# Weight blocks taken in pairs, and one home for both mixed inputs, in an attention and channel-mix kernel

## The chip, the cores and the metric

The kernel runs on one core of a Trainium2 chip. The metric is the device time in microseconds of one execution. The engines are TensorE (PE; its weight loads are PEld), VectorE (DVE), ScalarE (ACT), GpSimd (POOL) and SyncE (SP), which here issues nearly all DMAs from one queue, in order.

## The reference

Two stages. The first is attention for 4 batches, 8 heads, 768 rows and head dimension 64. The scores have a distance bias per head; a row sees the first 8 columns and the 96 columns up to itself. The second stage takes the 512 attention outputs of a row as x:

```
xk = mu_k * x + (1 - mu_k) * x_prev        # x_prev: the row before
xr = mu_r * x + (1 - mu_r) * x_prev
k  = max(xk @ w_k, 0)                      # w_k 512 x 1024
v  = (k * k) @ w_v                         # w_v 1024 x 512
r  = 1 / (1 + exp(-(xr @ w_r)))            # w_r 512 x 512
out = r * v
```

The weights arrive as 64-bit floating point and everything else as 32-bit.

## The kernel before

The 3072 rows are 24 tiles of 128. Each step takes one tile: scores, a maximum and an exponential per head, a sum and its reciprocal (L363, L364 on VectorE), normalisation on GpSimd (L367), a transpose (on TensorE, L404, for the first nine tiles; by VectorE and DMA after that), and the product with v (L425). A step has four slots; the program counts them as `4 * step + hp`. The second stage takes chunks of two tiles, 12 in all. A chunk is a generator with 40 pieces, and each slot asks for five of them, so TensorE alternates between attention and the chunk of some tiles before (the first chunk begins late in step 3). When the last attention step is done, the remaining pieces run back to back.

**The weights.** They are 20 blocks of 128 rows and 512 columns in the order w_k (8), w_r (4), w_v (8). A block goes through three steps.

- `weight_load` (L149): a DMA of the 64-bit words, 512 KB, into a home. The home is a buffer that has another use later: xk_hi, xr_hi, xk_lo, xr_lo (the mixed x), kk_hi and kk_lo (the squared k, two blocks in each), and the three t4k buffers. A home that is taken a second time must have been read out first.
- `weight_begin` (L168): the conversion to 32-bit words. One multiplication, on ScalarE for even blocks (L177) and on GpSimd for odd ones (L175), and then three integer operations on VectorE (L178, L179, L180), the last of which reads the home for the last time.
- `weight_split` (L182): a rounded high part by ScalarE or GpSimd (L187) and the low part by a subtraction on VectorE (L189 before the first output product exists, L192 behind it). The low part takes a buffer of the pool `wl`; the word's buffer comes free with that.

The first chunk multiplies plain 32-bit words (L495 for kp, L474 for z, L527 for the v products, `vps`). All later chunks use high and low parts, three matmuls for each product (L465 to L467). So the words must be there in time for the first chunk and the splits for the second. `w_due` (L147) lists how many blocks are to be loaded, and how many begun, by the end of each slot; `splits_ok` says how many may be split after each piece of the first chunk's v products.

**The chunk.** `mix` (L436) makes xk and xr for all chunks but the first, each as a high and a low tile; `plain_mix` (L448) makes the first chunk's. The tiles kk and sig of a chunk (L500, L478) share the pool `f2`; sig is what the output DMA (L535) reads. The tile framework gives every buffer of a pool to a new tile when all readers of the old one are done, and it orders the instructions of each engine when the program is built, by its own simulated timeline (L773); it does not reorder at run time. So each engine works through a fixed list.

Of the kernel before, what the change touches and what calls it, by code (L numbers as in the profile page):

```python
# [9 lines left out]
F32 = mybir.dt.float32  # L10
F32R = mybir.dt.float32r
# [23 lines left out]
def tile_biased_attention_channel_mix(ctx: ExitStack, tc: tile.TileContext, qT, kT, v, n_sizes, mu_kr, w_k, w_v, w_r, q_rows, k_rows, v_rows, slopes, out):  # L35
    nc = tc.nc
# [107 lines left out]
    w_steps = [(name, src, k, c) for name, src, kts, n in (("k", w_k, 4, DF), ("r", w_r, 4, DM), ("v", w_v, 8, DM)) for c in range(0, n, 512) for k in range(kts)]  # L144

    w_raw = {}
    w_due = ((2, 3, 4, 5, 6, 6, 7, 7, 8, 8, 9, 9, 10, 11, 12, 13, 14, 16, 18, 20, 20, 20, 20, 20), (0, 1, 2, 3, 4, 4, 5, 5, 6, 6, 7, 7, 8, 8, 9, 10, 11, 12, 14, 16, 18, 20, 20, 20))  # L147

    def weight_load(i):  # L149
        name, src, k, c = w_steps[i]  # L150
        home = w_homes[i]
        if home == "t4k":
            raw = p4k.tile([128, 512, 2], I32, tag="t4k", name=f"w64_{i}")
        elif home[0] == "x":
            raw = f_pool.tile([128, 512, 2], I32, tag=home, name=f"w64_{i}")
        else:
            if home in w_both:
                raw = w_both.pop(home)[:, 1]
            else:
                w_both[home] = f_pool.tile([128, 2, 512, 2], I32, tag=home, name=f"w64_{i}")  # L160
                raw = w_both[home][:, 0]
        nc.sync.dma_start(raw.rearrange("p n w -> p (n w)"), src[k * 128 : (k + 1) * 128, 2 * c : 2 * c + 1024])
        w_raw[i] = raw

    w_both = {}
    w_homes = ["xk_hi", "xr_hi", "xk_lo", "xr_lo", "kk_hi", "kk_hi", "kk_lo", "kk_lo"] + 2 * ["t4k", "t4k", "t4k", "xk_lo", "xr_lo"] + ["kk_lo", "kk_lo"]

    def weight_begin(i):  # L168
        name, src, k, c = w_steps[i]
        raw = w_raw.pop(i)  # L170
        low, top = raw[:, :, 0], raw[:, :, 1]
        word = w_pool.tile([128, 512], I32, tag="wl", name=f"word_{i}")
        w_word[name, k, c] = word.bitcast(F32)
# [6 lines left out]
        vec.scalar_tensor_tensor(word, low, 29, word, op0=ALU.logical_shift_right, op1=ALU.bitwise_or)  # L180

    def weight_split(i):  # L182

        name, src, k, c = w_steps[i]
        word, hi = w_word.pop((name, k, c)), w_hi[name][:, k, c : c + 512]
        lo = w_low[name, k, c] = w_pool.tile([128, 512], F32R, tag="wl", name=f"w{name}_lo_{i}")
        (act.copy if i % 4 < 2 else pool_copy)(hi, word)  # L187
        if not gates:
            vec.tensor_sub(lo, word, hi)  # L189
        else:  # L190
            with tc.issue_after(gates[-1]):
                vec.tensor_sub(lo, word, hi)  # L192
# [240 lines left out]
            act.copy(xt[:, :, 1 + 128 * i : 129 + 128 * i], s["av"].rearrange("p (a q) -> p a q", a=4))  # L433


    def mix(xc, xp, tag, tmp_pool, out_pool):  # L436
        m, m1 = mu[tag]
        tmp = tmp_pool.tile([128, 4, 256], F32, name=f"mix_{tag}", tag="t4k")
        hi = out_pool.tile([128, 4, 256], F32R, name=f"x{tag}_hi", tag=f"x{tag}_hi")
        lo = out_pool.tile([128, 4, 256], F32R, name=f"x{tag}_lo", tag=f"x{tag}_lo")  # L440
        for j in range(4):
            pool.tensor_scalar(tmp[:, j, :], xp[:, j, :], m1[:, j : j + 1], 1.0, op0=ALU.mult, op1=ALU.mult)
            vec.scalar_tensor_tensor(tmp[:, j, :], xc[:, j, :], m[:, j : j + 1], tmp[:, j, :], op0=ALU.mult, op1=ALU.add)
        act.copy(hi, tmp)
        vec.tensor_sub(lo, tmp, hi)
        return hi, lo

    def plain_mix(xc, xp, tag):  # L448

        m, m1 = mu[tag]  # L450
        x = f_pool.tile([128, 4, 256], F32, name=f"x{tag}_0", tag=f"x{tag}_hi")
        for j in range(4):
            act.activation(x[:, j, :], xp[:, j, :], AF.Copy, scale=m1[:, j : j + 1])
            vec.scalar_tensor_tensor(x[:, j, :], xc[:, j, :], m[:, j : j + 1], x[:, j, :], op0=ALU.mult, op1=ALU.add)
        return x

    def channel_mix(xk, xr, out_rows, f_pool, f2_pool, ps_f, first=False, last=False):
        if first:
# [22 lines left out]
        sigs = []  # L481
        for fp in range(4):
            if first:
                weights_go(4 if fp < 2 else 8)
            else:
                splits_go(4 if fp < 2 else 8)
            ps = ps_f.tile([128, 512], F32, name="kp", tag="f")
            for u in range(2):
                f = slice((2 * fp + u) * 128, (2 * fp + u + 1) * 128)
                c = fp // 2 * 512  # L490
                g = slice(f.start - c, f.stop - c)
                o = ps[:, u * 256 : (u + 1) * 256]
# [24 lines left out]
        for i in range(2):  # L517
            c = slice(i * 128, (i + 1) * 128)
            sig = sigs[i][1]
            w = 256 if last and i else 512  # L520
            for o in range(0, 512, w):
                d = slice(o, o + w)
                vp = ps_f.tile([128, 512], F32, name="vps", tag="f")
                for f in range(8):
                    if first:
                        weights_go(13 + f)
                        pe.matmul(vp, kk_all[:, f, c], w_word["v", f, 0], start=f == 0, stop=f == 7)  # L527
                        if i or f > 3:
                            splits_ok[0] = 13 + f if i else 12
                    else:  # L530
                        splits_go(13 + f)
# [81 lines left out]
    def wide():  # L613
        with ExitStack() as g:
# [85 lines left out]
            with tc.For_i(0, B, 1) as b:  # L700
                for c in range(3):
# [7 lines left out]
                    xk = mix(xt[:, :, 1:257], xt[:, :, 0:256], "k", work, work)  # L709
                    xr = mix(xt[:, :, 1:257], xt[:, :, 0:256], "r", work, work)  # L710
# [66 lines left out]
```

## Time and profile before

| | us |
|---|---|
| time, median of 3 runs | 483.69 (482.35 to 485.16) |
| profiled execution | 482.42 |
| its span, first to last instruction | 480.6 |
| TensorE busy in the span | 468.3 |
| VectorE busy | 380.6 |
| ScalarE busy | 283.0 |
| GpSimd busy | 255.5 |

Busy time adds what each engine spends in instructions. Matmuls are pipelined and their ends are modelled, so TensorE's busy time says where it had work rather than how hard it worked. [...] A wait is written as engine, line and tile that waited, an arrow, and what ended the wait.

### The profile page before, as it was taken

How to read it: one execution, taken by the hardware profiler on the slowest of the kernel's cores; microseconds unless marked ns; L12 is line 12 of the kernel's file. 1: busy time of each engine (PE TensorE's matmuls, PEld its weight loads, DVE VectorE, ACT ScalarE, POOL GpSimd, SP SyncE). 2: the span in 40 equal slices, each digit the busy share in tenths (PEclk: the TensorE clock that was granted, in tenths of full speed). 3: DMA queues.
4: the chain of work that ended last, by engine and by line, in shares of the span. 5: the costliest groups of instructions: out<-in, count | busy, mean ns of one | idle time of the engine just before them, and what ended most of it. 6: DMA issues, size and time to landing. Idle time of an engine off the chain costs nothing.

```text
span 480.6 us, 9646 instructions
## 1 busy us (share of the span) xinstructions
PE 468.3 (97%) x3300; PEld 402.7 (84%) x3300; DVE 380.6 (79%) x921; ACT 283.0 (59%) x656; POOL 255.5 (53%) x396
## 2 busy tenths in 40 slices
PE   8979999999999999999999999999999999999996
PEld 6758854788898898898898898898898898898985
DVE  6899999988778968978978968978978968746221
ACT  5996636367669548546738638636748549543220
POOL 7676977537447536737646645737646645303000
PEclk9999999999999999999999999999999999999999
DMA  6999634502422575865775785775775554430001
GB/s 177 309 297 312 234 80 64 144 11 89 110 66 72 155 214 177 225 192 143 192 219 182 230 227 165 219 211 159 195 202 191 172 183 160 160 109 24 22 2 48
DMA packets 42279, 76.20 MB, mean 159 GB/s; under 512 B 5616, under 2 KB 23280, under 8 KB 42224
## 3 DMA queue, kind: packets, MB, share of 16 engines
q1 hardware_dynamic: 42080, 75.52, 53.5%
q8 instruction: 28, 0.46, 0.4%
q14 instruction: 27, 0.22, 0.2%
q10 hardware_dynamic: 144, 0.00, 0.0%
HBM read 54.53 MB, written 20.97 MB: 157 GB/s over the span
## 4 chain that ended last, share of the span: by engine, by line
PE 84%; DVE 8%; POOL 2%; issue 2%; DMA 2%; SPq 0%; ACT 0%; POOLq 0%; DVEq 0%
PE vps L466 9%; PE vps L465 9%; PE vps L467 8%; PE kp L465 8%; PE av L425 8%; PE kp L467 8%; PE kp L466 8%; PE z L465 4%; PE z L466 4%; PE z L467 4%; PE s L327 4%; PE s L328 3%; PE t L404 2%; POOL room L367 2%; PE s L325 2%
## 5 line engine op out<-in xcount | busy, mean ns | idle before, releaser
L367 POOL TENSOR_SCALAR room<-room,r 128x256 f32<-128x256 f32 (+1 forms) x192 | 110.2, 591 | 141.7 <-DVE r L364 72.9
L351 ACT ACTIVATE room<-room,nmax 128x256 f32<-128x256 f32 (+1 forms) x192 | 93.0, 486 | 89.7 <-DVE nmax L350 84.2
L465 PE MATMUL kp<-xk_hi,wk_hi 128*128 128x256 f32 x352 | 99.4, 282 | 0.8 <-DVE kk L506 0.8
L467 PE MATMUL kp<-xk_hi,wk_lo 128*128 128x256 f32 x352 | 98.6, 280 | 0.0
L466 PE MATMUL kp<-xk_lo,wk_hi 128*128 128x256 f32 x352 | 98.2, 279 | 0.0
L350 DVE CUSTOM_DVE_ANT_0 room<-s,pat 128x256 f32<-128x256 f32 (+1 forms) x192 | 68.4, 389 | 3.8 <-PE s L325 2.4
L466 PE MATMUL vps<-wv_lo,kk_hi 128*128 128x512 f32 (+1 forms) x184 | 70.9, 385 | 0.0
L465 PE MATMUL vps<-wv_hi,kk_hi 128*128 128x512 f32 (+1 forms) x184 | 70.8, 385 | 0.0
L467 PE MATMUL vps<-wv_hi,kk_lo 128*128 128x512 f32 (+1 forms) x184 | 70.5, 383 | 0.0
L465 PEld LDWEIGHTS kp<-xk_hi,wk_hi 128*128 128x128 f32 x352 | 66.8, 190 | 1.9 <-DVE kk L506 1.0
L466 PEld LDWEIGHTS kp<-xk_lo,wk_hi 128*128 128x128 f32 x352 | 65.9, 187 | 0.7 <-issue 0.2
L467 PEld LDWEIGHTS kp<-xk_hi,wk_lo 128*128 128x128 f32 x352 | 66.0, 187 | 0.0
L378 DVE STREAM_TRANSPOSE room<-room 128x512 f32<-128x512 f32 x52 | 36.0, 702 | 18.0 <-POOL room L367 18.0
L508 DVE TENSOR_TENSOR kk_lo<-kk,kk_hi 128x512 fp32r<-128x512 f32 x44 | 33.7, 765 | 15.0 <-ACT kk_hi L507 13.5
L507 ACT CAST kk_hi<-kk 128x512 fp32r<-128x512 f32 x44 | 27.1, 617 | 26.7 <-DVE kk L506 26.7
L506 DVE TENSOR_TENSOR kk<-kp,kk 128x512 f32<-128x512 f32 x44 | 30.1, 685 | 14.4 <-ACT kk L502 14.3
L467 PEld LDWEIGHTS vps<-wv_hi,kk_lo 128*128 128x128 f32 x184 | 34.6, 188 | 7.5
L465 PEld LDWEIGHTS vps<-wv_hi,kk_hi 128*128 128x128 f32 x184 | 34.7, 188 | 6.4
L425 PE MATMUL av<-room,va 128*64 128x128 f32 x608 | 39.5, 277 | 0.4 <-ACT room L405 0.4
L466 PEld LDWEIGHTS vps<-wv_lo,kk_hi 128*128 128x128 f32 x184 | 34.5, 188 | 6.1
L425 PEld LDWEIGHTS av<-room,va 128*64 128x64 f32 x608 | 33.9, 136 | 5.7 <-issue 2.9
L327 PE MATMUL s<-kw,qh 128*128 128x256 f32 (+1 forms) x136 | 37.0, 295 | 0.0
(116 smaller groups left out, 1022.3 us busy)
## 6 DMA issues: line engine op xcount, KB each, us to landing
moved<-room SPq DMA_DIRECT2D x26, 512.0 KB, 4.0
room<-moved SPq DMA_DIRECT2D x104, 128.0 KB, 3.0
kraw<-in_kT_dram SPq DMA_DIRECT2D x36, 256.0 KB, 4.0
qraw<-in_qT_dram SPq DMA_DIRECT2D x34, 256.0 KB, 4.0
out_dram<-sig SPq DMA_DIRECT2D x23, 256.0 KB, 3.8
va<-in_v_dram SPq DMA_DIRECT2D x21, 256.0 KB, 3.4
w<-in_w_k_dram SPq DMA_DIRECT2D x8, 512.0 KB, 7.8
w<-in_w_v_dram SPq DMA_DIRECT2D x8, 512.0 KB, 4.3
```

The source lines that it names most:

```text
L327: pe.matmul(o, s["qh"][:, h, :], s["kw"][:, h, c0:256], start=True, stop=False)
L350: vec.tensor_tensor_reduce(out=e[:, :w], in0=o, in1=p[:, h, :], op0=ALU.add, op1=ALU.min, scale=-0.125, scalar=3.0e38, accum_out=s["nmax"] ...
L351: act.activation(e[:, :w], e[:, :w], AF.Exp, bias=s["nmax"][:, h : h + 1], scale=-1.0, accum_out=s["sum"][:, h : h + 1])
L367: pool.tensor_scalar(e[:, :w], e[:, :w], r[:, i : i + 1], 1.0, op0=ALU.mult, op1=ALU.mult)
L378: vec.transpose(dst, src.rearrange("p u (g b j) -> p (u g) b j", b=4, j=32))
L425: pe.matmul(o, vt[:, h * 64 : (h + 1) * 64], g, start=k == 0, stop=k == nb - 1)
L465: pe.matmul(o, sh, mh, start=first, stop=False)
L466: pe.matmul(o, sh, ml, start=False, stop=False)
L467: pe.matmul(o, sl, mh, start=False, stop=last)
L506: vec.tensor_mul(kk, pv, kk)
L507: act.copy(kkh[:, 2 * fp : 2 * fp + 2, :], kk)
L508: vec.tensor_sub(kkl[:, 2 * fp : 2 * fp + 2, :], kk, kkh[:, 2 * fp : 2 * fp + 2, :])
```

## The change

Weights go in ten pairs of blocks. A pair is two neighbouring blocks of rows in the same 512 columns: one DMA of 1 MB, one multiplication and three VectorE operations over 1024 columns, one rounding and one subtraction over 1024 columns. Even pairs take ScalarE for the multiplication and the rounding, odd pairs GpSimd. The pool `wl` has 11 buffers of twice the size, `f2` three instead of four. The mixed x has one tile x_hi of twice the size for the high parts of xk and xr, and one x_lo for the low parts. The pairs' homes are x_hi, x_lo, kk_hi, kk_lo, and then three times x_lo and kk_lo in turn; t4k is no home any more. The lists of due slots and the counts at which the chunks ask for weights are in pairs. The arithmetic is the same.

```diff
-    w_pool = ctx.enter_context(tc.tile_pool(name="wl", bufs=21))
+    w_pool = ctx.enter_context(tc.tile_pool(name="wl", bufs=11))
...
-    f2_pool = fast.enter_context(tc.tile_pool(name="f2", bufs=4))
+    f2_pool = fast.enter_context(tc.tile_pool(name="f2", bufs=3))
...
-    w_steps = [... for c in range(0, n, 512) for k in range(kts)]
+    w_steps = [... for c in range(0, n, 512) for k in range(0, kts, 2)]
...
-    w_due = ((2, 3, 4, 5, 6, 6, 7, 7, 8, 8, 9, 9, 10, 11, 12, 13, 14, 16, 18, 20, 20, 20, 20, 20), (0, 1, 2, 3, 4, 4, 5, 5, 6, 6, 7, 7, 8, 8, 9, 10, 11, 12, 14, 16, 18, 20, 20, 20))
+    w_due = ((1, 2, 2, 3, 3, 3, 3, 4, 4, 4, 5, 5, 5, 6, 6, 7, 8, 9, 10, 10, 10, 10, 10, 10), (0, 1, 1, 2, 2, 2, 2, 3, 3, 3, 4, 4, 4, 5, 5, 6, 7, 8, 9, 10, 10, 10, 10, 10))
+    w_homes = ["x_hi", "x_lo", "kk_hi", "kk_lo"] + 3 * ["x_lo", "kk_lo"]
...
     def weight_load(i):
+        raw = w_raw[i] = f_pool.tile([128, 2, 512, 2], I32, tag=w_homes[i], name=f"w64_{i}")
+        nc.sync.dma_start(raw.rearrange("p k n w -> p k (n w)"), src[k * 128 : (k + 2) * 128, 2 * c : 2 * c + 1024].rearrange("(k p) x -> p k x", k=2))
...
-    w_homes = ["xk_hi", "xr_hi", "xk_lo", "xr_lo", "kk_hi", "kk_hi", "kk_lo", "kk_lo"] + 2 * ["t4k", "t4k", "t4k", "xk_lo", "xr_lo"] + ["kk_lo", "kk_lo"]
...
     def weight_begin(i):
-        word = w_pool.tile([128, 512], I32, tag="wl", name=f"word_{i}")
+        word = w_pool.tile([128, 2, 512], I32, tag="wl", name=f"word_{i}")
...
     def weight_split(i):
-        lo = w_low[name, k, c] = w_pool.tile([128, 512], F32R, tag="wl", name=f"w{name}_lo_{i}")
-        (act.copy if i % 4 < 2 else pool_copy)(hi, word)
+        lo = w_pool.tile([128, 2, 512], F32R, tag="wl", name=f"w{name}_lo_{i}")
+        (act.copy if i % 2 == 0 else pool_copy)(hi, word)
...
-    def mix(xc, xp, tag, tmp_pool, out_pool):
+    def mixes(xc, xp, tmp_pool, out_pool):
+        both = [out_pool.tile([128, 2, 4, 256], F32R, name=f"x_{p}", tag=f"x_{p}") for p in ("hi", "lo")]
+        for i, tag in enumerate("kr"):
...
-    def plain_mix(xc, xp, tag):
+    def plain_mixes(xc, xp):
+        both = f_pool.tile([128, 2, 4, 256], F32, name="x_0", tag="x_hi")
+        for i, tag in enumerate("kr"):
...
-                            splits_ok[0] = 13 + f if i else 12
+                            splits_ok[0] = 6 + (f + 1) // 2 if i else 6
```

## Rows read from the trace of the kernel before

**Rows 1.** Page: engines' busy time, share of the span, instructions.
```profile
PE 468.3 (97%) x3300; PEld 402.7 (84%) x3300; DVE 380.6 (79%) x921; ACT 283.0 (59%) x656; POOL 255.5 (53%) x396
```
**Rows 2.** Windows: us, busy (instructions) of PE, PEld, DVE, ACT, POOL, clock, DMA, GB/s.
```profile
16.00:36.00 20.00, 15.97 (x132) 12.49 (x132) 18.86 (x61) 19.09 (x54) 14.36 (x19) 1.00 1.04 302
36.00:57.00 21.00, 20.98 (x144) 18.26 (x144) 21.00 (x56) 13.77 (x37) 15.42 (x21) 1.00 0.85 277
57.00:75.00 18.00, 18.00 (x94) 9.79 (x93) 17.39 (x28) 9.18 (x16) 14.59 (x16) 1.00 0.54 127
86.00:102.00 16.00, 14.81 (x139) 13.39 (x138) 14.90 (x38) 6.63 (x22) 6.89 (x12) 1.00 0.31 85
...
200.00:250.00 50.00, 50.00 (x386) 45.58 (x385) 41.90 (x99) 28.31 (x72) 27.31 (x41) 1.00 0.70 197
```
**Rows 3.** Waits of PE, whole span: us in total, times, longest.
```profile
PE t L404 <- POOL room L367: 4.0, 5, 1.4
...
PE kp L465 <- DVE kk L506: 0.8, 1, 0.8
...
PE vps L527 <- DVE word L180: 0.5, 1, 0.5
PE av L425 <- ACT room L405: 0.4, 1, 0.4
```
**Rows 4.** Timeline of DVE: start, us, engine, line, operation, tiles, shapes.
```profile
24.55 0.68 DVE L179 SCALAR_TENSOR_TENSOR word<-w,word 128x512 int32<-128x512 int32 x1
25.16 0.16 DVE L363 TENSOR_SCALAR r<-sum 128x4 f32<-128x4 f32 x1
...
43.51 0.66 DVE L180 SCALAR_TENSOR_TENSOR word<-w,word 128x512 int32<-128x512 int32 x1
...
82.21 1.22 DVE L445 TENSOR_TENSOR xk_lo<-mix_k,xk_hi 128x1024 fp32r<-128x1024 f32 x1
83.34 1.22 DVE L445 TENSOR_TENSOR xr_lo<-mix_r,xr_hi 128x1024 fp32r<-128x1024 f32 x1
```
**Rows 5.** Groups: ns min/median/max, then starts; or busy us, mean ns.
```profile
L175 POOL TENSOR_SCALAR word<-w x10: 651/789/1110, 16.8 to 65.7; 128x512 f32<-128x512 f32 x10
L192 DVE TENSOR_TENSOR wv_lo<-word,wv_hi x8: 685/691/822, 93.6 to 99.6; 128x512 fp32r<-128x512 f32 x8
...
L454 DVE SCALAR_TENSOR_TENSOR xk<-x,mus,xk 128x256 f32<-128x256 f32 x4 | 2.7, 702 | 0.0
```
**Rows 6.** SyncE's queue: its waits in all, and the timeline of the loads.
```profile
SPq L162 <- DVE word L180: 9.3, 5, 4.6
...
44.51 12.42 SPq L162 DMA_DIRECT2D w<-in_w_v_dram  x7
```
**Rows 7.** Weight loads from 44 to 58 us, to landing.
```profile
DMA to landing us min/median/max: 3.3/4.1/4.7
```
**Rows 8.** Timeline of POOL.
```profile
48.24 3.48 POOL L367 TENSOR_SCALAR room<-room,r 128x256 f32<-128x256 f32 x4
...
59.01 5.12 POOL L367 TENSOR_SCALAR room<-room,r 128x256 f32<-128x256 f32 x4
```
**Rows 9.** Timeline of PE, first chunk's v products; last column: idle before, releaser.
```profile
73.25 1.98 PE L527 MATMUL vps<-word,kk 128*128 128x512 f32 x4
...
75.89 1.13 PE L527 MATMUL vps<-word,kk 128*128 128x512 f32 x2 [0.55 <-DVE word L180]
```
**Rows 10.** One chunk in the steady part: PE, ACT, SP timelines, and the page's DMA issues.
```profile
223.67 0.40 PE L465 MATMUL z<-wr_hi,xr_hi 128*128 128x512 f32 x1
...
230.35 1.04 ACT L444 CAST xk_hi<-mix_k 128x1024 fp32r<-128x1024 f32 x1
...
241.73 0.43 SPq L535 DMA_DIRECT2D out_dram<-sig  x1
...
249.78 0.59 ACT L502 ACTIVATE kk<-kp 128x512 f32<-128x512 f32 x1
...
out_dram<-sig SPq DMA_DIRECT2D x23, 256.0 KB, 3.8
```

More of the change, by code (lines that the diff above doesn't have):

```diff
@@ L142, in tile_biased_attention_channel_mix @@
     pool.tensor_scalar(mus1, mus, -1.0, 1.0, op0=ALU.mult, op1=ALU.add)
-    w_steps = [(name, src, k, c) for name, src, kts, n in (("k", w_k, 4, DF), ("r", w_r, 4, DM), ("v", w_v, 8, DM)) for c in range(0, n, 512) for k in range(kts)]
+    w_steps = [(name, src, k, c) for name, src, kts, n in (("k", w_k, 4, DF), ("r", w_r, 4, DM), ("v", w_v, 8, DM)) for c in range(0, n, 512) for k in range(0, kts, 2)]
     w_raw = {}
-    w_due = ((2, 3, 4, 5, 6, 6, 7, 7, 8, 8, 9, 9, 10, 11, 12, 13, 14, 16, 18, 20, 20, 20, 20, 20), (0, 1, 2, 3, 4, 4, 5, 5, 6, 6, 7, 7, 8, 8, 9, 10, 11, 12, 14, 16, 18, 20, 20, 20))
+    w_due = ((1, 2, 2, 3, 3, 3, 3, 4, 4, 4, 5, 5, 5, 6, 6, 7, 8, 9, 10, 10, 10, 10, 10, 10), (0, 1, 1, 2, 2, 2, 2, 3, 3, 3, 4, 4, 4, 5, 5, 6, 7, 8, 9, 10, 10, 10, 10, 10))
+    w_homes = ["x_hi", "x_lo", "kk_hi", "kk_lo"] + 3 * ["x_lo", "kk_lo"]
     def weight_load(i):
         name, src, k, c = w_steps[i]
[L151 to L165, printed above, removed]
-    w_homes = ["xk_hi", "xr_hi", "xk_lo", "xr_lo", "kk_hi", "kk_hi", "kk_lo", "kk_lo"] + 2 * ["t4k", "t4k", "t4k", "xk_lo", "xr_lo"] + ["kk_lo", "kk_lo"]
+        raw = w_raw[i] = f_pool.tile([128, 2, 512, 2], I32, tag=w_homes[i], name=f"w64_{i}")
+        nc.sync.dma_start(raw.rearrange("p k n w -> p k (n w)"), src[k * 128 : (k + 2) * 128, 2 * c : 2 * c + 1024].rearrange("(k p) x -> p k x", k=2))
     def weight_begin(i):
@@ L170, in weight_begin @@
         raw = w_raw.pop(i)
-        low, top = raw[:, :, 0], raw[:, :, 1]
-        word = w_pool.tile([128, 512], I32, tag="wl", name=f"word_{i}")
-        w_word[name, k, c] = word.bitcast(F32)
+        low, top = raw[:, :, :, 0], raw[:, :, :, 1]
+        word = w_pool.tile([128, 2, 512], I32, tag="wl", name=f"word_{i}")
+        w_both[i] = word.bitcast(F32)
+        for j in range(2):
+            w_word[name, k + j, c] = w_both[i][:, j]
         if i % 2:
@@ L180, in weight_begin @@
         vec.scalar_tensor_tensor(word, low, 29, word, op0=ALU.logical_shift_right, op1=ALU.bitwise_or)
+    w_both = {}
     def weight_split(i):
         name, src, k, c = w_steps[i]
-        word, hi = w_word.pop((name, k, c)), w_hi[name][:, k, c : c + 512]
-        lo = w_low[name, k, c] = w_pool.tile([128, 512], F32R, tag="wl", name=f"w{name}_lo_{i}")
-        (act.copy if i % 4 < 2 else pool_copy)(hi, word)
+        word, hi = w_both.pop(i), w_hi[name][:, k : k + 2, c : c + 512]
+        lo = w_pool.tile([128, 2, 512], F32R, tag="wl", name=f"w{name}_lo_{i}")
+        for j in range(2):
+            w_low[name, k + j, c] = lo[:, j]
+        (act.copy if i % 2 == 0 else pool_copy)(hi, word)
         if not gates:
@@ L433, in weighted @@
             act.copy(xt[:, :, 1 + 128 * i : 129 + 128 * i], s["av"].rearrange("p (a q) -> p a q", a=4))
-    def mix(xc, xp, tag, tmp_pool, out_pool):
[L437 to L446, printed above, removed]
@@ L448, in plain_mix @@
-    def plain_mix(xc, xp, tag):
[L450 to L455, printed above, removed]
+    def mixes(xc, xp, tmp_pool, out_pool):
+        both = [out_pool.tile([128, 2, 4, 256], F32R, name=f"x_{p}", tag=f"x_{p}") for p in ("hi", "lo")]
+        for i, tag in enumerate("kr"):
+            m, m1 = mu[tag]
+            tmp = tmp_pool.tile([128, 4, 256], F32, name=f"mix_{tag}", tag="t4k")
+            hi, lo = (x[:, i] for x in both)
+            for j in range(4):
+                pool.tensor_scalar(tmp[:, j, :], xp[:, j, :], m1[:, j : j + 1], 1.0, op0=ALU.mult, op1=ALU.mult)
+                vec.scalar_tensor_tensor(tmp[:, j, :], xc[:, j, :], m[:, j : j + 1], tmp[:, j, :], op0=ALU.mult, op1=ALU.add)
+            act.copy(hi, tmp)
+            vec.tensor_sub(lo, tmp, hi)
+            yield hi, lo
@@ L457, in channel_mix @@
+    def plain_mixes(xc, xp):
+        both = f_pool.tile([128, 2, 4, 256], F32, name="x_0", tag="x_hi")
+        for i, tag in enumerate("kr"):
+            m, m1 = mu[tag]
+            x = both[:, i]
+            for j in range(4):
+                act.activation(x[:, j, :], xp[:, j, :], AF.Copy, scale=m1[:, j : j + 1])
+                vec.scalar_tensor_tensor(x[:, j, :], xc[:, j, :], m[:, j : j + 1], x[:, j, :], op0=ALU.mult, op1=ALU.add)
+            yield x
     def channel_mix(xk, xr, out_rows, f_pool, f2_pool, ps_f, first=False, last=False):
@@ L483, in channel_mix @@
             if first:
-                weights_go(4 if fp < 2 else 8)
+                weights_go(2 if fp < 2 else 4)
             else:
-                splits_go(4 if fp < 2 else 8)
+                splits_go(2 if fp < 2 else 4)
             ps = ps_f.tile([128, 512], F32, name="kp", tag="f")
@@ L509, in channel_mix @@
         if first:
-            weights_go(12)
+            weights_go(6)
         else:
-            splits_go(12)
+            splits_go(6)
         for i in range(2):
@@ L525, in channel_mix @@
                     if first:
[L526 removed]
+                        weights_go(7 + f // 2)
                         pe.matmul(vp, kk_all[:, f, c], w_word["v", f, 0], start=f == 0, stop=f == 7)
                         if i or f > 3:
[L529 removed]
+                            splits_ok[0] = 6 + (f + 1) // 2 if i else 6
                     else:
[L531 removed]
+                        splits_go(7 + f // 2)
                         three(vp[:, d], kkh[:, f, c], kkl[:, f, c], w_hi["v"][:, f, d], w_low["v", f, 0][:, d], f == 0, f == 7)
@@ L541, in ffn @@
         if c:
-            xk, xr = (mix(xt[:, :, 1:257], xt[:, :, 0:256], tag, p4k, f_pool) for tag in "kr")
+            xk, xr = mixes(xt[:, :, 1:257], xt[:, :, 0:256], p4k, f_pool)
         else:
-            xk, xr = (plain_mix(xt[:, :, 1:257], xt[:, :, 0:256], tag) for tag in "kr")
+            xk, xr = plain_mixes(xt[:, :, 1:257], xt[:, :, 0:256])
         return channel_mix(xk, xr, lambda i: out[(2 * c + i) * 128 : (2 * c + i + 1) * 128, :], f_pool, f2_pool, ps_f, c == 0, c == NCHUNK - 1)
@@ L708, in wide @@
                         nc.sync.dma_start(xt[:, :, 1:257], src[:, :, 0:256])
-                    xk = mix(xt[:, :, 1:257], xt[:, :, 0:256], "k", work, work)
-                    xr = mix(xt[:, :, 1:257], xt[:, :, 0:256], "r", work, work)
+                    xk, xr = mixes(xt[:, :, 1:257], xt[:, :, 0:256], work, work)
                     def out_rows(i):
```

## The prediction, made before the change was run

> **What bounds the kernel now.** I read the page's busy times first [rows 1], then a table of stretches [rows 2], then TensorE's waits [rows 3], and only then the order of single instructions. TensorE is busy 468.3 of 480.6 us, and in the steady part (200 to 250 us) it is busy 50.00 of 50.00 [rows 1, 2]. What the change touches lies almost wholly before 102 us. There the table shows two engines full at once: VectorE 21.00 of 21.00 us from 36 to 57 and 17.39 of 18 from 57 to 75, TensorE 20.98 and 18.00 in the same stretches. So VectorE time saved there is worth only what TensorE now waits for. Those waits are listed: 4.0 us of transposes waiting for GpSimd's normalisation (all of it in the stretch 16 to 36, where TensorE is busy 15.97 of 20), 0.8 for a kk of VectorE, 0.5 for a converted weight, 0.4 for a copy of ScalarE [rows 3]. Sum 5.7 us, 1.2% of the run: no gain can be larger. A loss has no such bound. After 102 us every microsecond that TensorE has lost before is simply added to the end.
>
> **The change part by part.** The sum is made against the profiled execution: 482.42 us, its span 480.6 and 1.8 around it. The median of the runs shown is 483.69, 1.27 higher; I add that at the end.
>
> *Fewer, longer VectorE instructions.* Twenty blocks of 512 columns take four each (three of the conversion, one subtraction), 80 in all; ten pairs take 40 of 1024 columns. An operation of 512 columns holds VectorE for 0.61 us (L179 starts at 24.55, the next instruction at 25.16), one of 1024 for 1.13 (L445 at 82.21, the next at 83.34) [rows 4]. A pair saves 2 x 0.61 - 1.13 = 0.09 us, and 40 of them 3.6 us of VectorE. L178 of 1024 columns doesn't occur before; I give it the same 0.09 (between 0, if nothing is shared, and its whole second start of 0.6).
> The row of one 512-column subtraction says 691 ns, that of 1024 says 1.22 us [rows 4, 5]. [...] But successive starts in this trace overlap the ends, so the 3.6 of the starts stands.
>
> *What of it reaches TensorE.* In the last stretch, 86 to 102 us, VectorE (14.90 of 16) runs the subtractions that are queued behind the first output product: 16 blocks now, since only four are emitted before it. In the change four pairs are emitted before it and six remain: 6 x 1.13 = 6.8 us instead of 16 x 0.61 = 9.8. The kk that TensorE waits for (0.8) and the copy before it (0.4) come 3 us sooner: -1.2 us. What is late next there: nothing that the trace shows.
>
> *The early stage (16 to 36 us).* The 4.0 us are set by reciprocals on VectorE and by GpSimd. Saved there: three pairs at 4 x 0.09, about 1.1 us of VectorE. Against it, a reciprocal that gets behind a conversion can now wait up to 1.13 instead of 0.61 us, and GpSimd's multiplication of a pair takes 2 x 0.79 = 1.6 us in one piece [rows 5]. The schedule also asks for the second block of pairs 2 and 3 up to two slots sooner. Bounds: -1.1, and +2.7 (each of the five waits longer by 0.52). I take 0, between them, as neither side has a row that decides.
>
> *The loads and their homes.* The bytes stay. Now the first eleven blocks have a home that no other weight holds, and later ones also use three t4k buffers. In the change there are four homes, and x_lo and kk_lo carry pairs 4 to 9 in turn: load 5 waits until pair 3 is converted, 7 until 5, 9 until 7. That wait exists already: SyncE's weight loads wait 9.3 us for the last conversion step in five cases [rows 6]. The new one is longer by its chain. Behind it on SyncE's queue stand the loads of tile 6 and v of tile 4 (both first used in step 6, after the first chunk's products) and 32 rows of v for step 5; those land some 6 us later than now and are used after 60 us, so nothing else is held up.
> Priced from the rows: both blocks of pair 3 are read out at 43.51 + 0.66 = 44.2 now, and the load that goes into their home is issued at 44.51 [rows 4, 6]. A load of 512 KB lands in 4.1 us there [rows 7]; the other 0.52 MB at 277 GB/s takes 1.9, so load 5 lands at 50.5. GpSimd multiplies the odd pairs and is in normalisations to 51.7 [rows 8]; its 1.6 us end at 53.3; three operations of at most 1.13 end at 56.7. Load 7 lands at 62.7, GpSimd is taken from 59.01 to 64.13 [rows 8], pair 7 is done at 69.1, load 9 lands at 75.1, pair 9 is done at 80.1. Its first use is the third of the four matmuls that start at 73.25 [rows 9], about 74.2. So 5.9 us late, where TensorE now waits 0.5 at 75.89.
> Two things shorten that. Pair 3 is due one slot earlier for its load and two for its conversion, so it goes ahead of the first chunk's mix on VectorE; the four operations of its k half take 2.7 us [rows 5], and with a part of the r half I estimate up to 4. And the next eight products (the second row half) need the same pairs 6 to 8 first: about 12 matmuls of 0.46 us, 5.5 us, that the planner can put ahead if it sees the wait. Bounds: -0.5 (the present wait gone) and +5.4. I take +1.5: the mix order gained, a part of the filling work used.
> The row gives 4.1 us for 512 KB. [...]
>
> *Three f2 buffers instead of four.* Kk number three of a chunk now waits for the second output of the chunk before. The output is issued at 241.73 and lands 3.8 us later, 245.5; the Relu that needs the buffer starts at 249.78 [rows 10]. 4.2 us of cover. Cost 0; without the cover ScalarE would stand by the difference, with five PSUM buffers behind it.
>
> *One tile for both mixed x.* The copy into the shared high half waits for the last z product rather than the last kp product. That z starts at 223.67 and the copy at 230.35 [rows 10]: 6 us of cover, cost 0.
>
> Sum: -1.2 + 0 + 1.5 + 0 + 0 = +0.3 us, 482.7 for a profiled execution; with 1.27 on it, 484.0.
>
> **The rivals.** *Faster, 480.0.* The planner hides the home wait, and VectorE's relief also reaches the reciprocals: -1.2, the 0.5 for the weight gone, and half of the early 4.0: -3.7. For it: VectorE is the full engine from 16 us on. Against it: the early waits are GpSimd's too, and the chain of homes is longer.
> *Slower, 487.9: the kk_lo chain decides.* Pair 3 is not converted sooner, and TensorE's order is not changed: +5.4 - 1.2 = +4.2. It bites once pair 3 is read out after 44.2 - 5.9 = 38.3 us. For it: the present order already ends with a wait at that place [rows 3, 9], and GpSimd is in long normalisations at both points. Against: the earlier due slots and the 5.5 us of filling work.
> *Slower, 486.7: coarse pieces.* Longer conversions push the reciprocals of the first four tiles back by the 0.52 us that each can lose, five times: +2.7 + 1.5 - 1.2 = +3.0.
>
> **How the numbers follow.** About 0.5% (2.4 us) is what a measurement of this kernel can tell from no change. The forecast with its own range of 481.5 to 486.0 gets 0.38; the faster rival 0.30; the home chain 0.21 and the coarse pieces 0.11, together 0.32 on the slower side. The range takes in both ends of the early stage and nearly the whole chain: 479.2 (a little beyond the faster rival, whose bound would be 478.0) to 488.8 (the chain with one queueing delay more).
>
> **What would show it.** Right: TensorE's wait at its first-chunk v products between 0.5 and 3 us, the last weight load issued between 60 and 70 us, no wait for a kk near 101, steady stretches still full. Wrong to the fast side: transposes waiting under 3 us before 36 and no weight wait. Wrong to the slow side: one wait of over 4 us at the first chunk's v products near 75 us, with SyncE holding the last loads until after 68. Wrong altogether: a TensorE gap after 110 us, which would make the two small buffer edits matter.

## The result: 489.67 us, slower

| | before | after |
|---|---|---|
| time, median of 4 runs, us | 483.54 (482.35 to 485.16) | 489.67 (487.85 to 490.66) |
| ratio | | 1.012 [1.0083, 1.0157] |
| profiled execution, us | 482.42 | 487.85 |
| its span, us | 480.6 | 486.1 |
| TensorE busy, us | 468.3 | 468.5 |
| VectorE busy, us | 380.6 | 375.3 |
| ScalarE busy, us | 283.0 | 280.5 |
| GpSimd busy, us | 255.5 | 255.8 |

The changed kernel is 1.2% slower, some 5.8 us (4.0 to 7.6), and 0.9 us above the end of the forecast's range. VectorE lost 40 instructions and 5.3 us of work, as meant. TensorE's busy time is the same to 0.2 us, and it stands idle 5.3 us longer.

### The profile page after: what moved, and what is told of

It reads as the page before. It is cut to its first block, busy times and chain, and to the rows that moved or that the text cites. A ratio compares the mean times of both kernels' runs of the same rounds, so it can differ in the third digit from the quotient of the medians.

```text
span 486.1 us, 9574 instructions
## 1 busy us (share of the span) xinstructions
PE 468.5 (96%) x3300; PEld 402.8 (83%) x3300; DVE 375.3 (77%) x881; ACT 280.5 (58%) x646; POOL 255.8 (53%) x386
## 4 chain that ended last, share of the span: by engine, by line
PE 83%; DMA 9%; DVE 4%; POOL 1%; issue 1%; SPq 1%; ACT 0%; POOLq 0%; DVEq 0%
PE kp L461 9%; PE kp L463 9%; PE kp L462 8%; PE vps L462 8%; PE vps L461 8%; PE vps L463 8%; PE av L418 7%; PE z L461 4%; PE z L462 4%; PE z L463 4%; PE s L320 4%; PE s L321 3%; DMA w<-in_w_k_dram 3%; DMA w<-in_w_v_dram 3%; PE vps L523 2%; DMA w<-in_w_r_dram 2%
## 5 line engine op out<-in xcount | busy, mean ns | idle before, releaser
L461 PE MATMUL kp<-x_hi,wk_hi 128*128 128x256 f32 x352 | 99.4, 282 | 0.0
L463 PE MATMUL kp<-x_hi,wk_lo 128*128 128x256 f32 x352 | 98.6, 280 | 0.0
L462 PE MATMUL kp<-x_lo,wk_hi 128*128 128x256 f32 x352 | 98.2, 279 | 0.0
L461 PEld LDWEIGHTS kp<-x_hi,wk_hi 128*128 128x128 f32 x352 | 66.8, 190 | 1.1 <-issue 0.4
L462 PEld LDWEIGHTS kp<-x_lo,wk_hi 128*128 128x128 f32 x352 | 65.9, 187 | 0.7 <-issue 0.2
L463 PEld LDWEIGHTS kp<-x_hi,wk_lo 128*128 128x128 f32 x352 | 66.0, 188 | 0.0
L371 DVE STREAM_TRANSPOSE room<-room 128x512 f32<-128x512 f32 x52 | 36.0, 702 | 17.9 <-POOL room L360 17.9
## 6 DMA issues: line engine op xcount, KB each, us to landing
w<-in_w_k_dram SPq DMA_DIRECT2D x4, 1024.0 KB, 11.1
```

What stands on the lines that cost most here:

```text
L371: vec.transpose(dst, src.rearrange("p u (g b j) -> p (u g) b j", b=4, j=32))
L461: pe.matmul(o, sh, mh, start=first, stop=False)
L462: pe.matmul(o, sh, ml, start=False, stop=False)
L463: pe.matmul(o, sl, mh, start=False, stop=last)
```

## The profile after

The lines of the changed kernel are numbered anew: the load is L153, the multiplications L164 (GpSimd) and L166 (ScalarE), the three conversion steps L167 to L169, the splits' subtraction L182, the first chunk's v products L523. First TensorE's waits over the whole span: total, times, longest.

```profile
PE vps L523 <- DVE word L169: 4.2, 1, 4.2
PE s L317 <- DVE word L167: 2.2, 1, 2.2
PE s L318 <- DMA ring<-in_kT_dram: 1.4, 2, 0.8
...
PE av L418 <- ACT room L398: 0.6, 1, 0.6
PE t L397 <- POOL room L360: 0.6, 1, 0.6
```

Against [rows 3]: the transposes' 4.0 us fell to 0.6 and the 0.8 for a kk is gone. But the converted weight, 0.5 before, now costs 4.2, and there are new waits at the scores (L317, L318).

The same stretches as in [rows 2] (busy time and instructions of PE, PEld, DVE, ACT, POOL; granted clock; DMA share; GB/s), with the one from 75 to 86 added:

```profile
16.00:36.00 20.00, 16.09 (x129) 13.51 (x127) 18.25 (x47) 16.10 (x45) 14.13 (x15) 0.91 1.01 281
36.00:57.00 21.00, 19.61 (x134) 16.72 (x135) 17.44 (x38) 12.86 (x30) 13.30 (x16) 1.00 0.61 196
57.00:75.00 18.00, 17.41 (x94) 10.06 (x93) 12.76 (x24) 10.84 (x19) 9.17 (x9) 1.00 0.75 224
75.00:86.00 11.00, 6.81 (x29) 3.32 (x28) 11.00 (x19) 3.33 (x10) 11.00 (x9) 0.84 0.36 57
86.00:102.00 16.00, 15.98 (x112) 11.51 (x111) 15.88 (x27) 5.57 (x14) 8.55 (x11) 1.00 0.35 88
...
200.00:250.00 50.00, 50.00 (x368) 44.72 (x367) 42.81 (x100) 27.70 (x69) 29.41 (x43) 1.00 0.72 195
```

Three things are to be seen. VectorE, full from 36 to 75 us before, now has 8.8 us free there: it waits for weights instead of being behind (7.5 us of that for GpSimd's multiplication L164). TensorE's granted clock was 1.00 in every stretch of [rows 2]; now it is 0.91 and 0.84 in two stretches. And the steady part is as full as before.

Where the 5.5 us of span arise is read from four places in TensorE's order: first kp of the first chunk, its first z, its first v product, first kp of the second chunk (kp, z and v products are the three groups of matmuls of a chunk).

| stretch | before, us | after, us | difference |
|---|---|---|---|
| start to first kp | 36.35 | 37.55 | +1.2 |
| to first z | 20.93 | 20.90 | 0 |
| to first v product | 11.14 | 11.95 | +0.8 |
| to first kp of the second chunk | 17.40 | 22.00 | +4.6 |
| to the end of the span | 394.78 | 393.70 | -1.1 |

*The v products.* This is the chain that ends at 80.67 us, timeline rows of several engines in order of time (start, us, engine, line, operation, tiles; idle before and its releaser at the end):

```profile
36.33 0.47 DVE L450 SCALAR_TENSOR_TENSOR x<-x,mus,x 128x256 f32<-128x256 f32 x1
37.42 3.04 DVE L450 SCALAR_TENSOR_TENSOR x<-x,mus,x 128x256 f32<-128x256 f32 x6
40.38 1.21 DVE L169 SCALAR_TENSOR_TENSOR word<-w,word 128x1024 int32<-128x1024 int32 x1
41.66 0.39 SPq L153 DMA_DIRECT2D w<-in_w_r_dram  x1
45.77 3.72 POOL L360 TENSOR_SCALAR room<-room,r 128x256 f32<-128x256 f32 x4 [2.87 <-ACT room L344]
49.46 1.14 POOL L164 TENSOR_SCALAR word<-w 128x1024 f32<-128x1024 f32 x1
53.53 1.35 DVE L169 SCALAR_TENSOR_TENSOR word<-w,word 128x1024 int32<-128x1024 int32 x1
54.96 11.25 SPq L153 DMA_DIRECT2D w<-in_w_v_dram  x3
59.92 1.12 POOL L164 TENSOR_SCALAR word<-w 128x1024 f32<-128x1024 f32 x1 [3.53 <-DMA w<-in_w_v_dram]
70.40 2.74 PE L523 MATMUL vps<-word,kk 128*128 128x512 f32 x6
73.23 1.12 POOL L164 TENSOR_SCALAR word<-w 128x1024 f32<-128x1024 f32 x1 [1.10 <-DMA w<-in_w_v_dram]
73.41 2.74 PE L523 MATMUL vps<-word,kk 128*128 128x512 f32 x6
74.38 0.97 DVE L167 TENSOR_SCALAR word<-word 128x1024 int32<-128x1024 int32 x1 [3.42 <-POOL word L164]
75.27 1.21 DVE L182 TENSOR_TENSOR wk_lo<-word,wk_hi 128x1024 fp32r<-128x1024 f32 x1
76.40 1.41 DVE L168 SCALAR_TENSOR_TENSOR word<-w,word 128x1024 int32<-128x1024 int32 x1
77.73 1.21 DVE L182 TENSOR_TENSOR wk_lo<-word,wk_hi 128x1024 fp32r<-128x1024 f32 x1
78.87 0.61 DVE L437 SCALAR_TENSOR_TENSOR mix_k<-x,mus,mix_k 128x256 f32<-128x256 f32 x1
79.41 1.21 DVE L169 SCALAR_TENSOR_TENSOR word<-w,word 128x1024 int32<-128x1024 int32 x1
80.67 3.59 PE L523 MATMUL vps<-word,kk 128*128 128x512 f32 x4 [4.19 <-DVE word L169]
```

L450 is the first chunk's mix: seven of its eight steps stand ahead of pair 3's last operation (its second one starts at 34.95). Pair 3 is read out at 41.6, and 0.07 us later load 5 is issued into its home; GpSimd, in a normalisation until 49.46, multiplies it then. The three loads of the row at 54.96 are those of pairs 7, 8 and 9. The landing of loads 5, 7 and 9, from the groups of line L153 in three short stretches:

```profile
L153 SPq DMA_DIRECT2D w<-in_w_r_dram x1: 394/394/394, 41.7 to 41.7; - x1
DMA to landing us min/median/max: 5.7/5.7/5.7
...
L153 SPq DMA_DIRECT2D w<-in_w_v_dram x1: 368/368/368, 55.0 to 55.0; - x1
DMA to landing us min/median/max: 4.9/4.9/4.9
...
L153 SPq DMA_DIRECT2D w<-in_w_v_dram x1: 368/368/368, 65.8 to 65.8; - x1
DMA to landing us min/median/max: 7.3/7.3/7.3
```

So load 9 lands at 73.1. From there the conversion takes until 80.62: the multiplication until 74.4, then the three operations, which would be done at 77.8 at 1.13 us each. The other 2.8 us come from two subtractions and a step of the mix that stand between them in VectorE's list. So of the wait of 4.2 us, 1.4 would be left without them (an estimate from these rows). TensorE has done only the products of pairs 6 to 8 for the first row half (the two rows of six records, two records to a product); the second half's stand behind the wait here, in program order. SyncE's weight loads wait 25.3 us in all for L169, in five cases, against 9.3 in [rows 6].

*The early stage.* SyncE's queue from 9 us on. Timeline of the kernel before:

```profile
9.45 2.89 SPq L162 DMA_DIRECT2D w<-in_w_k_dram  x5
12.39 0.70 SPq L246 DMA_DIRECT2D qz<-in_qT_dram  x1
```

And after, with the matmuls that need these loads:

```profile
9.45 1.48 SPq L153 DMA_DIRECT2D w<-in_w_k_dram  x3
10.97 0.85 SPq L239 DMA_DIRECT2D qz<-in_qT_dram  x1
...
24.11 0.92 PE L317 MATMUL s<-ring,qz 128*128 128x128 f32 x4 [2.17 <-DVE word L167]
25.83 0.68 PE L318 MATMUL s<-ring,qz 128*128 128x128 f32 x2 [0.80 <-DMA ring<-in_kT_dram]
```

The q loads issued between 10 and 15 us (group of the tile qz), before and then after:

```profile
DMA to landing us min/median/max: 9.6/10.0/10.4
```
```profile
DMA to landing us min/median/max: 12.5/12.8/13.0
```

Three pairs are 3 MB ahead of tile 3's q and k, where five blocks were 2.5 MB. The q loads are issued 1.4 us sooner and land later: the first, issued at 10.97, lands 13.0 later, at 24.0, just when the scores start. The wait at 24.11 is put down to VectorE by the profile; the releaser named is the event that came last before it, and three experiments below (s_single, s_splits, s_dummy) name the q load at the same place.

*The clock.* Windows of 1 us around the two long waits:

```profile
26.00:27.00 1.00, 1.00 (x6) 1.00 (x6) 1.00 (x1) 0.08 (x1) 1.00 (x1) 0.50 1.05 387
...
82.00:83.00 1.00, 1.00 (x2) 0.36 (x2) 1.00 (x6) 1.00 (x5) 1.00 (x2) 0.50 0.00 0
84.00:85.00 1.00, 1.00 (x14) 0.70 (x14) 1.00 (x2) 0.18 (x1) 1.00 (x2) 1.00 0.08 16
```

Behind each the granted clock is 0.50 for some 3.4 us. Four records of the v product take 3.59 us at 80.67, against 1.98 in [rows 9]: 1.6 us lost beside the wait itself. The stretch means say about the same: 0.09 of 20 us and 0.16 of 11 us are 1.8 each.

## Experiments

Two theories for the loss. A: the home chain of the odd pairs (3, 5, 7, 9) makes the v wait. B: three pairs ahead of tile 3's loads make the early waits. The rival is C: the merged operations are too coarse. Each edit is against the kernel named; times are medians. Ratios go against the kernel before in the same session, with a 95% interval; they are not the quotients of the two medians, and microseconds between kernels of different sessions are taken from them.

**s_small**, the kernel before with `f2` of three buffers and the shared tiles for the mixed x:

```diff
-    f2_pool = fast.enter_context(tc.tile_pool(name="f2", bufs=4))
+    f2_pool = fast.enter_context(tc.tile_pool(name="f2", bufs=3))
...
+        both = [out_pool.tile([128, 2, 4, 256], F32R, name=f"x_{p}", tag=f"x_{p}") for p in ("hi", "lo")]
```

> The kernel before with the two small edits alone: three f2 buffers instead of four, and one x_hi and one x_lo tile for both mixed x (the single 512-column blocks keep their 16 homes' order, two blocks to a tile). Theory (the pairs' chain through x_lo and kk_lo, 41.6 to 80.6 us in the changed kernel, and the slow clock behind it make the loss): 483.5, within 1 us of before, no wait of TensorE after 102 us. Rival (the small buffers cost it): 487 or more, with new waits for kk or x.

484.53 against 483.43, 1.0011 [0.9984, 1.0038]. No cost of the two small edits can be told.

**s_merge**, the kernel before with only the splits (rounding and subtraction) in pairs, and `wl` and `f2` as after:

```diff
-        (act.copy if i % 4 < 2 else pool_copy)(hi, word)
+        (act.copy if i % 2 == 0 else pool_copy)(hi, word)   # both blocks of a pair
```

> The kernel before with single loads, homes and conversions, but the rounding and the subtraction done on pairs of 1024 columns (ten splits instead of twenty; wl 11 pair buffers, three f2). Theory: the merged splits themselves gain; TensorE's waits at 89 and 101 us (0.4 and 0.8) go, 482.3. Rival (longer VectorE pieces hold up other work): 484.5 or more, with transposes waiting longer.

486.91 against 483.43, 1.0044 [1.0011, 1.0078]: a miss, with the longer transposes' wait that the rival names. The kk wait is gone, that for a copy of ScalarE is 1.6 us instead of 0.4, and one wait for a normalisation has grown, with a fall of the clock behind it (timeline, then windows of 4 us):

```profile
35.17 0.44 PE L410 MATMUL t<-ident,room 128*128 128x128 f32 x2 [2.79 <-POOL room L373]
```
```profile
36.00:40.00 4.00, 4.00 (x15) 3.27 (x15) 4.00 (x12) 3.19 (x9) 2.08 (x3) 0.50 1.03 326
```

The waits for normalisations sum to 4.8 us, against 4.0 in [rows 3], but the longest is 2.79 where it was 1.4, and some 10 us at half clock follow: 5 us of full clock are missing (the mean from 36 to 57 us is 0.76).

**s_single**, the changed kernel with its loads, homes and due slots, but every operation in blocks of 512 columns again:

```diff
-        vec.tensor_scalar(word, word, 3, 0x7FFFFFF8, ...)
+        for j in range(2):
+            wj, tj, lj = word[:, j], top[:, j], low[:, j]
+            vec.tensor_scalar(wj, wj, 3, 0x7FFFFFF8, ...)
...
```

> The changed kernel with its 1 MB loads, homes, due slots and pools, but the multiplication, the three conversion operations, the rounding and the subtraction in blocks of 512 columns (the multiplication alternating between ScalarE and GpSimd inside a pair). Theory: the chain of homes is the same, so TensorE's wait at the v products stays, 3 to 5 us, and VectorE has 3.6 us more: 488 to 491. Rival (the merged operations cost it): 484 to 486.

488.53 against 483.43, 1.0082 [1.0053, 1.0112]. By the ratios 4.0 of the 5.8 us are there without any merged operation, so C isn't the main cause; the 1.8 between them are within the intervals. TensorE's longest wait is 2.8 us for `qz<-in_qT_dram`, as B says; the v wait is 1.5.

**s_homes**, the changed kernel with pairs 4, 6 and 9 in two t4k buffers each and only pair 7 behind pair 3 in kk_lo:

```diff
-    w_homes = ["x_hi", "x_lo", "kk_hi", "kk_lo"] + 3 * ["x_lo", "kk_lo"]
+    w_homes = ["x_hi", "x_lo", "kk_hi", "kk_lo", "t4k", "x_lo", "t4k", "kk_lo", "x_lo", "t4k"]
```

> The changed kernel with other homes: pairs 4, 6 and 9 go block by block through the three t4k buffers (converted in single blocks), pair 5 and 8 through x_lo, pair 7 through kk_lo; so the longest chain has three pairs with room between. Theory: the last weight load is issued some 10 us sooner, the wait at the v products and the slow clock after it are gone: 5 us less than the changed kernel, 484 to 485. Rival (coarse pieces or the early stage make the loss): 488 to 490.

488.44 against 483.43, 1.0091 [1.0062, 1.012]: a miss in time. The v wait is gone from the trace, as A says, but it shows early waits of 1.27, 0.89, 0.86, 0.98 and 1.32 us, and about 10 us at half clock behind the last one. The four places tell where the time went: from the first v product to the second chunk it takes 16.66 us (17.40 before, 22.00 after), so what A names is gone; the first kp comes at 39.79 and the first z 23.53 later, 6.0 us more than before together. The edit leaves the three pairs ahead of tile 3's loads.

**s_due**, the changed kernel with the loads of pairs 2 and 3 one slot later, behind the loads of tiles 3 and 4:

```diff
-    w_due = ((1, 2, 2, 3, 3, 3, 3, 4, 4, 4, ...
+    w_due = ((1, 2, 2, 2, 3, 3, 3, 3, 4, 4, ...
```

> The changed kernel with the loads of pairs 2 and 3 one slot later, so that they stand behind the loads of tiles 3 and 4 on SyncE's queue. Theory (3 MB of weights ahead of tile 3 make its scores late at 24 to 26 us, and TensorE's clock falls to half after that wait): the waits at 24 to 26 us and the slow stretch after them go, 1.2 + 1.7 us: 486.5 to 487. The wait at the v products stays. Rival (the early waits come from the long VectorE pieces alone): the wait for VectorE of 2.2 us at 24 us stays, 489 to 490.

486.99 against 484.33, 1.0046 [1.0016, 1.0076], some 3.6 us better than the changed kernel (the two intervals allow about 1 to 6). The q loads now land after 10.2 to 10.8 us, no score waits for them, and the first kp starts at 34.97. The rest of the loss is later (the profiled execution, 483.95, is one of the shortest):

```profile
74.37 3.70 PE L523 MATMUL vps<-word,kk 128*128 128x512 f32 x8
78.34 1.02 PE L523 MATMUL vps<-word,kk 128*128 128x512 f32 x2
82.35 0.38 PE L462 MATMUL kp<-x_lo,wk_hi 128*128 128x256 f32 x1 [1.48 <-DVE x_lo L439]
88.33 3.70 PE L523 MATMUL vps<-word,kk 128*128 128x512 f32 x8 [1.64 <-DVE word L169]
```

Here TensorE's list is another one. The products of pairs 6 to 8 for both row halves (24 of the 32 records) and the first kp of the second chunk stand ahead of pair 9's four products, the row at 88.33. Load 9 lands at 70.4, but VectorE's three operations for pair 9 are spread from 78.05 to 88.28.

**s_act**, the changed kernel with pairs 5, 7 and 9 multiplied on ScalarE, which shortens the chain by the wait for GpSimd and alters no load before 16 us:

```diff
-        if i % 2:
+        if i % 2 and i < 5:
             pool.tensor_scalar(word.bitcast(F32), top.bitcast(F32), 2.0**-112, 1.0, ...)
```

> The changed kernel with the multiplication of pairs 5, 7 and 9 on ScalarE instead of GpSimd. Theory (the chain pair 3 - 5 - 7 - 9 through kk_lo sets the wait at the v products): pair 5's multiplication no longer waits 2.0 us behind a normalisation (landed 47.4, multiplied from 49.46), so the 4.2 us wait falls to about 2: 487 to 488. Rival (something else than this chain holds pair 9): wait and time unchanged, 489.7.

486.16 against 484.33, 1.0046 [1.0014, 1.0078], also some 3.6 us better, with as wide an interval. The mirror image of s_due: the early wait stays, the v wait shrinks from 4.19 to 0.76 (profiled execution 483.56, the shortest), and the stretch from the first v product to the second chunk takes 17.46 us, as before the change.

```profile
24.63 1.15 PE L317 MATMUL s<-ring,qz 128*128 128x128 f32 x4 [2.69 <-DVE r L357]
...
79.87 1.98 PE L523 MATMUL vps<-word,kk 128*128 128x512 f32 x4 [0.76 <-DVE word L169]
```

The chain is shorter as meant: load 9 lands at 68.7 instead of 73.1. But pair 9 is done at 79.82, only 0.8 us sooner, as VectorE's three operations for it are spread over 8.8 us. The rest of the shorter wait is TensorE's: it begins the v products 0.7 us later, and a product of the second row half and some scores now stand ahead of the wait. So the run shows that the wait goes with the loss, not that the chain alone made it.

**s_splits**, the changed kernel with two pairs instead of six allowed to be split while the first row half's products are emitted, so that the subtractions between pair 9's steps go:

```diff
-                            splits_ok[0] = 6 + (f + 1) // 2 if i else 6
+                            splits_ok[0] = 6 + (f + 1) // 2 if i else 2
```

> The changed kernel with only two pairs split before the first output product instead of four. Theory: VectorE's subtractions that stand between pair 9's three conversion steps (75.27 and 77.73, 1.13 us each) move behind the gate; the 4.2 us wait falls to about 2, the last stretch before 102 us gets 2.3 us more VectorE work: 487.5 to 489. Rival (the steps wait for the load alone): unchanged, 489.7.

488.61 against 484.33, 1.008 [1.005, 1.011]. The v wait is gone from its trace, yet 8.4 us of full clock are missing (the mean is 0.83 from 16 to 36 us and 0.76 from 36 to 57) behind early waits of 2.4 us for a q load and up to 1.5 for a k load. As the waits that the edit doesn't touch changed too, the time says nothing on the split order alone. Pair 9 is done at 78.39, 2.2 us sooner than in the changed kernel, and the v products begin at 74.48, 4.1 us later: what is lost ahead of them shortens the v wait.

**s_dummy**, the changed kernel with 36 matmuls of zeros, into a buffer that nothing reads, ahead of pair 9's first product:

```diff
+                        if f == 6 and i == 0:
+                            for _ in range(36):
+                                pe.matmul(idle2[:, 0:256], zeros[:, 0:128], zeros, start=True, stop=True)
```

> The changed kernel with 36 matmuls of zeros into an unused PSUM tile ahead of the v product that waits for pair 9 (about 4 us of TensorE work at 0.11 us each; the output doesn't use them). Theory (part of the loss is TensorE's slow clock after the wait, 3.4 us at half speed): pair 9 comes as late as before, but the clock stays at 1.00 behind it, 1.7 us gained: 488. Rival (the clock has no part in it): 489.7 or more.

492.36 against 484.33, 1.0153 [1.0114, 1.0192]: a miss, though not told apart from the changed kernel's 1.012. The zeros take 4.1 us of TensorE and leave a wait of 1.2 for pair 9. The granted clock behind it is 1.00, and the four records that took 3.59 us take 1.99. But the wait for the q load is 4.2 here, and two for copies of ScalarE make 3.5. So the time doesn't tell what the clock alone costs.

**c_due_act**, the edits of s_due and s_act together:

```diff
+    w_due = ((1, 2, 2, 2, 3, 3, 3, 3, 4, 4, ...
...
+        if i % 2 and i < 5:
```

> The changed kernel with both single edits that helped: loads of pairs 2 and 3 one slot later (behind tiles 3 and 4), and the multiplications of pairs 5, 7 and 9 on ScalarE. Theory (two separate causes: tile 3 late behind 3 MB of weights, and the kk_lo chain): each gave back about 3.6 us alone, together the kernel is back at the kernel before, ratio 0.997 to 1.002. Rival (one cause seen twice, or the gains overlap): ratio 1.004 to 1.005 as with each alone.

485.03 against 483.78, 1.0012 [0.9988, 1.0037]. Both edits together bring back the time of the kernel before. By the ratios the excess is 5.8 us for the changed kernel, 2.2 with either edit and 0.6 (-0.6 to 1.8) with both. So there are two causes that can be taken away one by one: each is worth some 3.6 us alone, and together they are worth less than that sum. Its profiled execution was one of its longest, 487.57 of 482.55 to 487.57, and shows what is left in such a one:

```profile
25.33 1.78 PE L418 MATMUL av<-room,early 128*64 128x128 f32 x14 [3.39 <-DMA early<-in_v_dram]
...
88.85 6.16 PE L523 MATMUL vps<-word,kk 128*128 128x512 f32 x8 [2.69 <-DVE word L169]
```

Now v is the late load, not q or k. The eight records that wait are pair 9's products for both row halves, as in s_due: load 9 lands at 71.6 and pair 9 is done at 88.8, behind other work in VectorE's list. So a quicker chain of homes isn't what this trace shows; both edits also brought other lists, in which TensorE has more to do ahead of that wait.

**c_due_homes**, s_due with the homes of s_homes:

```diff
+    w_due = ((1, 2, 2, 2, 3, 3, 3, 3, 4, 4, ...
...
+    w_homes = ["x_hi", "x_lo", "kk_hi", "kk_lo", "t4k", "x_lo", "t4k", "kk_lo", "x_lo", "t4k"]
```

> The changed kernel with the later loads of pairs 2 and 3 and the other homes (pairs 4, 6 and 9 block by block through t4k). Theory: neither the tile-3 wait nor the chain is left: ratio 0.997 to 1.002, no wait of over 1.5 us before 102 us. Rival (long VectorE pieces in the early stage remain and bring the slow clock): ratio 1.005 or more.

487.69 against 483.78, 1.006 [1.0032, 1.0088]: a miss. Its waits are 3.1 us for a copy of ScalarE, 2.5 for a load of v and 1.7 for a converted weight. So other homes are no remedy as they stand, though s_homes shows no v wait; what brings these waits was not followed further.

**c_due_act_single**, c_due_act with every operation in blocks of 512 columns, as in s_single:

```diff
+            if j and i < 5:
+                pool.tensor_scalar(wj.bitcast(F32), tj.bitcast(F32), 2.0**-112, 1.0, ...)
...
```

> As the kernel with later loads and ScalarE's multiplications, but all conversions, roundings and subtractions in blocks of 512 columns. It tells what merging itself is worth where loads and chain are mended. Theory (merging gives VectorE back some 3.6 us, of which little reaches TensorE): 0 to 2 us slower than with merged operations. Rival (coarse pieces cost in the early stage more than they save): 1 to 3 us faster than with merged operations.

490.17 against 483.78, 1.0154 [1.0114, 1.0194]: 5 us more than c_due_act by the medians and 7 by the ratios, where 0 to 2 were expected. Without the merged operations the v wait is 3.3 us, one transpose waits 2.0, and the mean clock is 0.80 from 36 to 57 us. That is more than the 3.6 us of VectorE that merging saves; what of it is the operations' own and what the new order of all lists isn't shown.

**b_load**, the kernel before with six blocks (3 MB) instead of five ahead of tile 3's loads:

```diff
-    w_due = ((2, 3, 4, 5, 6, 6, 7, ...
+    w_due = ((2, 4, 4, 6, 6, 6, 7, ...
```

> The kernel before with one edit: six blocks (3 MB) of weights are loaded ahead of tile 3 instead of five, as in the changed kernel. Theory (the order of loads alone makes tile 3 late): a wait for qz or ring of 1 to 2.5 us at 22 to 26 us, in part with a slow clock behind it: 1.5 to 3.5 us slower than before. Rival (the long VectorE pieces make the early wait): same as before within 1 us.

486.35 against 483.78, 1.0055 [1.0029, 1.008]. B is shown from the other side: the load order alone costs the kernel before 2.7 us (1.4 to 3.9). Its q loads land after 11.1 to 11.2 us instead of 9.6 to 10.4. In its trace the k loads are waited for 2.4 us in all (0.7 before), and the longest wait for a normalisation is 3.57 us (1.4 before), with a mean clock of 0.86 from 36 to 57 us behind it:

```profile
26.10 0.49 PE L325 MATMUL s<-ring,qz 128*128 128x128 f32 x2 [1.16 <-DMA ring<-in_kT_dram]
...
35.98 1.37 PE L404 MATMUL t<-ident,room 128*128 128x128 f32 x4 [3.57 <-POOL room L367]
```

The landing of the first half of tile 3's q goes with this in all fourteen traces. With 2 MB of weights ahead of it (s_due and the three c_ kernels) it lands at 21.3 to 22.8 us, with 2.5 MB (before, s_small, s_merge) at 22.4 to 22.8, and with 3 MB (the other seven) at 23.6 to 26.0.

No version was faster than the kernel before.

## Why the prediction was wrong

The forecast was +0.3 us for the profiled execution, and it is +5.4. Term by term:

- **The loads and their homes: +1.5 taken, +4.6 measured** (17.40 against 22.00 us from the first v product to the second chunk). This is the step that failed: both things that I set against the chain. That pair 3 "goes ahead of the first chunk's mix on VectorE" held for two of its three operations only; seven of the eight mix steps ran ahead of the last, and pair 3 was read out at 41.6, 2.6 us sooner than before where up to 4 was reckoned, and 3.3 after the rival's point of decision, 38.3. And the second row half's products, which "the planner can put ahead", stood behind the wait: the 5.5 us were there and none was used. From pair 3 on the chain ran as worked out: load 7 landed at 59.9 (62.7 predicted), load 9 at 73.1 (75.1), pair 9 was done at 80.6 (80.1), as the head start of 2 us was lost again at pair 9, whose three operations took 6.2 us instead of 3.4. The wait is 4.2. And it has a price behind it that no term had: 1.6 us at half clock. How the 4.2 us divide between the chain of homes and VectorE's order stays open: the rows above leave 1.4 to the chain, and s_act, whose load 9 came 4.4 us sooner, had pair 9 only 0.8 sooner.
- **The early stage: 0 taken, +1.2 measured** in the profile, and more in the medians: taking it away gave some 3.6 us (s_due), adding it to the kernel before cost 2.7 (b_load). It is within the bounds of -1.1 to +2.7, but by luck: the mechanism was not mine. I weighed reciprocals behind longer conversions, and that the second block of a pair comes sooner, for VectorE and GpSimd; what a sixth block does to the loads of tile 3 behind it on SyncE's queue I did not follow. The transposes' wait that I watched did fall, from 4.0 to 0.6.
- **The last stretch: -1.2 taken, -1.1 measured.** The kk wait of [rows 3] is gone, and so is the copy before it.
- **Between z and v products: nothing taken, +0.8 measured**, of which 0.6 is a wait for a copy of ScalarE (L398).
- **f2, one tile for both mixed x: 0 taken.** No wait of either shows in the trace, and s_small gives 1.0011.
- **VectorE's relief: 3.6 us taken.** The successive starts that it rests on hold: L182 at 75.27, the next at 76.40, 1.13 us. The 5.3 us by which the busy time fell add durations, whose ends overlap the next start, so they don't contradict it.

So the rival "the kk_lo chain decides" (487.9, chance 0.21) was right in place and nearly in size, and the early stage came on top of it.

The landings of the chain agree with the sum in total but not one by one: loads 5, 7 and 9 took 5.7, 4.9 and 7.3 us, 17.9 together, against three times 6.0. Other loads of 1 MB were quicker: the five that s_due issues from 42 us on took 4.7 to 5.1 us.

"Coarse pieces" was wrong as the main cause: s_single keeps 4.0 of the 5.8 us without them. That s_merge is slower by 0.44% remains unexplained beyond its one wait of 2.79 us and the clock behind it.

## What to carry to other kernels

A coarser load is a change of the queue's order: for every DMA that now stands behind it, add the bytes ahead of it and compare its landing with its first use (here 12.8 us to landing behind 3 MB of weights, 10.0 behind 2.5). A chain of reused homes is to be walked to its last link before its cost is set against work that a planner "can" put ahead. Whether it does is to be read from the list itself: in the changed kernel none of those products stood ahead of the wait, in s_act one, in s_due all six. A wait of one engine for another is a difference of two times, and time lost earlier shortens it; so two causes in a row need not add up. And a wait of TensorE is priced with the clock that may follow it: one of 2.8 us in s_merge was followed by some 10 us at half clock, and five of 0.4 to 1.4 in the kernel before by none.

## What the runs showed of the hardware

TensorE's granted clock fell to 0.50 behind single waits of 2.2 and 0.8 us close together (after, 24 to 26 us), 2.8 (s_merge) and 4.2 us (after), and also behind five waits of 0.9 to 1.3 us in s_homes; it stayed at 1.00 through five waits of 1.4 us or less in the profiled execution of the kernel before. The stretches at half clock were about 3.4 us in the changed kernel and about 10 us in s_merge and s_homes, so 1.7 or 5 us of full clock are missing behind the same kind of wait. Why one stretch is longer than another was not settled. What is missing is not all lost: in s_small 1.7 us are missing from 36 to 57 us behind a wait of 2.6, and that execution took 482.73 us. In s_merge longer executions go with a lower mean clock, from 483.40 us at 0.992 to 489.09 at 0.985; in s_splits the shortest, 486.04, has 0.980 and one of 490.04 has 0.987. So the clock goes with a part of the spread, not with all of it.
